# Where the 448-column operands of TensorE lie in SBUF: at multiples of 256 bytes, or 64 bytes behind them

## The chip, the cores and the metric

The kernel runs on one core of one Trainium2 chip. The metric is the device time of one execution, in microseconds. The kernel before took 874.99 us, the median of three runs (873.45 to 876.74).

## The reference

Two layers, each a linear attention block and a dense block, are applied in turn to `x` of 2048 tokens by 448 features; both layers use the same weights. All is float32.

```python
def _A_ref(x, wqkv, wo):                       # 16 heads of 28
    q, k, v = ...                              # x @ wqkv, 448 x 1344
    pq, pk = phi(q), phi(k)                    # where(t > 0, t + 1, exp(t)) + 1e-6
    kv = jnp.einsum("bhsd,bhse->bhde", pk, v)
    z = jnp.einsum("bhsd->bhd", pk)
    num = jnp.einsum("bhqd,bhde->bhqe", pq, kv)
    den = jnp.einsum("bhqd,bhd->bhq", pq, z)[..., None] + 1e-6
    return (num / den) merged @ wo

def _B_ref(x, w1, b1, w2, b2):                 # 448 -> 1792 -> 448
    return gelu(x @ w1 + b1) @ w2 + b2

x = x + _A_ref(_layernorm(x), A_wqkv, A_wo)
x = x + _B_ref(_layernorm(x), B_w1, B_b1, B_w2, B_b2)
# and both once more
```

## The kernel before, in words

**Splitting.** The products are made in the float32r type. Each operand is split into a high part, rounded to that type, and a low part, the rest; a product is then high x high, high x low and low x high. Tiles whose names end in h or hi and l or lo are such pairs (`w1h`/`w1l`, `w2h`/`w2l`, `gh`/`gl`, `kh`/`kl`, `XH`/`XL`, `Mh`/`Ml`).

**Tiling.** The tokens lie in 16 tiles of 128, a tile of `x` being 128 x 448. In the attention block each tile is normalized, transposed by blocks through DRAM (or, for the first tiles, by TensorE) into `XH` and `XL`, and projected to K and Q: 11 matmuls each, with 128 x 128 pieces of XH or XL as the stationary operand and 448 columns of the weights `wk` or `wq` as the moving one (`proj`, L555). The G matmuls (L625) add up the transposed normalized input times phi(K) over all tiles, in four PSUM banks, again with 448 columns of `kh` or `kl` moving. From G, `wv` and `wo` small products give a matrix M (`kv`, `m`), and each output tile is phi(Q) times M: 448 columns of M move (`o`, `oc`; `oc` reads M from the tiles of the used-up `wq`, filled by DMA). In the dense block, blocks of four tiles (512 tokens) are multiplied by `w1`: here 512 columns of XH or XL move, as four runs of 128 (`f_`, L902). Gelu follows on ScalarE, the split on ScalarE and VectorE, and then for each of the 14 pieces of 128 hidden features the product with `w2`: 448 columns of `w2h` or `w2l` move over 128 x 128 pieces of `gh` or `gl` (`y_mm`, L931).

**Order.** The order of the work on all engines is written out by hand: `ORDER` (L15) has for each layer a text of short names with tile numbers, and `run` (L973) issues them one after the other. The prefix `>` marks work of the next layer. Dependencies between engines become semaphore waits by the tiles read and written.

**Buffers.** SBUF tiles come from the pools `consts`, `smalls`, `wts` and `work`, one behind the other. `work` holds rings, one for each tag (`ring`, L167), with as many buffers as `BUFS` (L155) says: H (9 buffers of 448 columns: tiles of x and pieces of wv), S (5 of 1024: staging, spread tiles, the pieces of wo, `Ml`), W0 to W6 and V0 to V6 (pieces of `wk` and `wq`, later phi(Q) and others), E and F (2 each of 512: `kh`, `kl`, `zh`, `zl`, `Mh`, later halves of phi(Q)), A and B (2 each of 512: `gh`, `gl`, `xnh`, `xnl`), e, xn, XH, XL, tail. The pool `wts` holds `w1h`, `w1l`, `w1x`, `w2h`, `w2l`.

**Addresses.** `consts` and `smalls` end at byte 6144 of a partition, which is 24 x 256, and every tile of `wts` and `work` is a multiple of 256 bytes long (448 columns are 7 x 256 bytes, 512 columns 8 x 256). So in the kernel before, every moving and every stationary operand of the matmuls of 448 and of 512 columns starts at a multiple of 256, but for a handful with `ones` or quarters of a tile as the stationary one.

Of the kernel before, what the change touches and what calls it, by code (L numbers as in the profile page):

```python
# [8 lines left out]
F32 = mybir.dt.float32  # L9
F32R = mybir.dt.float32r  # L10
# [111 lines left out]
def linear_attn_mlp_kernel(  # L122
# [15 lines left out]
    S, D = x0.shape  # L138
    F = w1.shape[1]
    H, DH = 16, 28  # L140
    NT = S // 128
    NF = F // 128
    G = 112
# [5 lines left out]
    smalls = ctx.enter_context(tc.tile_pool(name="smalls", bufs=2))  # L149
    wts = ctx.enter_context(tc.tile_pool(name="wts", bufs=1))  # L150
    work = ctx.enter_context(tc.tile_pool(name="work", bufs=2))
    psum = ctx.enter_context(tc.tile_pool(name="psum", bufs=1, space=bass.MemoryType.PSUM))
    ctx.enter_context(tc.manual_schedule())

    BUFS = {"H": 9, "S": 5, "e": 3, "xn": 2, "A": 2, "B": 2, "E": 2, "F": 2, "X": 2, "tail": 2, "small": 2}  # L155
# [5 lines left out]
    def f(ap):  # L161
        return ap.bitcast(F32)
# [2 lines left out]
        return psum.tile([128, 512], F32, name=name, tag=tag, bufs=BANKS[tag])  # L165

    def ring(tag, n, name, dt=F32):  # L167
        return work.tile([128, n], dt, name=name, tag=tag, bufs=BUFS.get(tag, 1))

    def wide(tag):  # L170
        return 512 if tag in ("xn", "W4", "W5") else D
# [32 lines left out]
    w1h = wts.tile([128, 3, F], F32R, name="w1h")  # L204
    w1l = wts.tile([128, 3, F], F32R, name="w1l")
    w1x = wts.tile([128, F], F32R, name="w1x")
    w2h = wts.tile([128, NF, D], F32R, name="w2h")
    w2l = wts.tile([128, NF, D], F32R, name="w2l")

    def rows(t):  # L210
        return slice(t * 128, (t + 1) * 128)
# [1 line left out]
    T = {}  # L213
# [8 lines left out]
    def copy(eng, out, src):  # L222
        if eng is act:
            act.copy(out, src)  # L224
        else:
            eng.tensor_copy(out, src)
# [37 lines left out]
    def load_half(src, h, name):  # L264
        s = ring("S", 1024, name)[:, :2 * D].rearrange("p (c n) -> p c n", c=2)
        if h == 0:
            sp.dma_start(s, src[:256, :].rearrange("(c p) n -> p c n", p=128))
        else:
            sp.dma_start(s[:, 0], src[256:TL, :])
            sp.dma_start(s[:64, 1], src[TL:, :])  # L270
            sp.dma_start(s[64:, 1], src[TL:, :])
        return s

    def wpiece(name, i):
        tag = f"{'W' if name == 'k' else 'V'}{i}"
        return ring(tag, wide(tag), f"w{name}{i}", F32R)[:, :D]

    def wload(name, col):
        def go(l, n, e):
            if l:  # L280
                T[l, "st", name, n] = load_half(wqkv[:, col:col + D], n, "stg")
                return
            if (l, "st", name, n // 2) not in T:
                T[l, "st", name, n // 2] = ring("S", 1024, "stg")[:, :2 * D].rearrange("p (c n) -> p c n", c=2)
            load_piece(wqkv[:, col:col + D], n, T[l, "st", name, n // 2][:, n % 2], ENG[e or "s"])
        return go
# [301 lines left out]

    @op
    def kh(l, t, e):  # L590
        T["kh", l, t] = ring("E", 512, "kh", F32R)[:, :D]
        T["kl", l, t] = ring("F", 512, "kl", F32R)[:, :D]
        act.activation(T["kh", l, t], T["K", l, t], AF.Identity, bias=tiny)

    @op
# [28 lines left out]
    @op  # L624
    def G_(l, t, e):  # L625
        if t == 0:
            T["G", l] = [bank("acc", f"G{c}")[:, :D] for c in range(4)]
        acc = T["G", l]
        h, lo = T["sp", l, t]
        kh, kl = T["kh", l, t], T["kl", l, t]  # L630
        first, last = t == 0, t == NT - 1
        for c in range(4):
            pe.matmul(acc[c], h[:, c * 128:(c + 1) * 128], kh, start=first, stop=False)
        for c in range(4):
            pe.matmul(acc[c], h[:, c * 128:(c + 1) * 128], kl, start=False, stop=last and c == 3)
        for c in range(3):
            pe.matmul(acc[c], lo[:, rows(c)], kh, start=False, stop=last)
# [29 lines left out]

    @op
    def zh(l, n, e):
        T[l, "zh"] = ring("E", 512, "zh", F32R)[:, :D]  # L670
        copy(ENG[e or "a"], T[l, "zh"], T["za", l])

    @op
    def zl(l, n, e):
        T[l, "zl"] = ring("F", 512, "zl", F32R)[:, :D]
        dve.tensor_sub(T[l, "zl"], T["za", l], f(T[l, "zh"]))

    @op
# [56 lines left out]

    @op
    def mh(l, g, e):
        T[l, "Mh", g] = ring("EEFF"[g], 512, "Mh", F32R)[:G, :D]
        copy(ENG[e or "a"], T[l, "Mh", g], T[l, "mp", g])

    @op
# [268 lines left out]
```

## Time and profile before

| | |
|---|---|
| time, median of 3 runs | 874.99 us (873.45 to 876.74) |
| profiled execution, its own time | 874.72 us |
| its span, first to last instruction | 873.0 us |
| TensorE (PE) busy | 99%, 4144 matmuls |
| weight loads (PEld) busy | 88%, 4144 loads |
| VectorE, ScalarE, GpSimd busy | 52%, 41%, 24% |
| granted TensorE clock | 0.999 |

PE rows are matmuls and PEld rows the loads of their stationary operands, which overlap them. Matmuls also overlap one another, and their ends are modelled, so a row's mean length is longer than the distance from one start to the next. In a row that groups instructions, the name after `<-` lists what the instruction reads: first the moving operand, then the stationary one (`y<-w2h,gh` moves w2h over gh, `hp<-XH,w1h` moves XH over w1h). Then come the shape, the count, the busy time of the group, the mean length of one in ns, and the idle time before them with what ended it.

### The profile page before, as it was taken

To read this page: it belongs to the slowest core of one execution; us is meant where nothing else is said; L and a number is where in the kernel's file an instruction comes from. 1 tells how busy PE (TensorE), PEld (TensorE's weight loads), DVE (VectorE), ACT (ScalarE), POOL (GpSimd) and SP (SyncE) were. 2 spreads that over 40 slices of the span, in tenths; PEclk is the share of its full clock that TensorE was granted. 3 is DMA by queue.
4 is the path that set the end of the run, shared out by engine and by line. 5 is a ranking of instruction groups with operands and counts; after the bars stand their busy time and mean duration, and the time that the engine had idled before them with its cause. 6 is when DMAs were issued, how large, how long until landed. Compare 5 with 4: busy or idle time off the path is not lost. (4 is left out here: it accounts for less than half of the span.)

```text
span 873.0 us, 11506 instructions
## 1 busy us (share of the span) xinstructions
PE 865.5 (99%) x4144; PEld 768.3 (88%) x4144; DVE 451.2 (52%) x893; ACT 356.5 (41%) x618; POOL 213.5 (24%) x277
## 2 busy tenths in 40 slices
PE   9999999999999999999999999999999999999998
PEld 7999998898888888888899989879888888888887
DVE  7986786574442442235288757846565414332112
ACT  7667646433223213333355664544142332222222
POOL 4655753434110012000122343232222000310000
PEclk9999999999999999999999999999999999999999
DMA  7685366743242113021154534571612402110101
GB/s 222 208 251 174 117 202 217 219 132 124 75 155 70 40 45 118 1 95 60 48 175 147 195 96 139 163 233 28 207 61 97 133 3 88 60 48 1 43 1 42
DMA packets 66392, 98.93 MB, mean 113 GB/s; under 512 B 9248, under 2 KB 60960, under 8 KB 66336
## 3 DMA queue, kind: packets, MB, share of 16 engines
q1 hardware_dynamic: 64528, 98.20, 35.1%
q8 instruction: 32, 0.52, 0.2%
q10 hardware_dynamic: 1808, 0.01, 0.1%
q14 instruction: 24, 0.20, 0.1%
HBM read 58.27 MB, written 36.70 MB: 109 GB/s over the span
## 5 line engine op out<-in xcount | busy, mean ns | idle before, releaser
L929 DVE TENSOR_TENSOR gl<-g,gh 128x512 fp32r<-128x512 f32 x112 | 77.5, 700 | 260.5 <-ACT gh L224 229.6
L919 ACT ACTIVATE g<-hp,b1s 128x512 f32<-128x512 f32 x112 | 76.6, 688 | 329.9 <-PE hp L914 316.3
L938 PE MATMUL y<-w2h,gh 128*128 128x448 f32 x448 | 163.7, 365 | 0.0
L939 PE MATMUL y<-w2l,gh 128*128 128x448 f32 x448 | 163.6, 365 | 0.0
L909 PE MATMUL hp<-XH,w1h 128*128 128x512 f32 x336 | 131.6, 392 | 1.6 <-ACT g L919 1.6
L910 PE MATMUL hp<-XH,w1l 128*128 128x512 f32 x336 | 131.2, 390 | 0.0
L370 POOL TENSOR_TENSOR brs<-bmv,mhalf 128x1 f32<-128x1 f32 x64 | 36.8, 579 | 330.2 <-DVE bmv L364 325.0
L941 PE MATMUL y<-w2h,gl 128*128 128x448 f32 x448 | 116.8, 365 | 0.0
L913 PE MATMUL hp<-XL,w1h 128*128 128x512 f32 x336 | 94.4, 389 | 0.0
L939 PEld LDWEIGHTS y<-w2l,gh 128*128 128x128 f32 x448 | 84.2, 188 | 8.0
L938 PEld LDWEIGHTS y<-w2h,gh 128*128 128x128 f32 x448 | 84.1, 188 | 8.0
L224 ACT CAST gh<-g 128x512 fp32r<-128x512 f32 x112 | 68.5, 620 | 54.4 <-PE y L939 46.3
L941 PEld LDWEIGHTS y<-w2h,gl 128*128 128x128 f32 x448 | 84.1, 188 | 6.9
L909 PEld LDWEIGHTS hp<-XH,w1h 128*128 128x128 f32 x336 | 63.1, 188 | 14.0 <-ACT g L919 2.0
L913 PEld LDWEIGHTS hp<-XL,w1h 128*128 128x128 f32 x336 | 63.1, 188 | 13.2
L910 PEld LDWEIGHTS hp<-XH,w1l 128*128 128x128 f32 x336 | 63.1, 188 | 11.9
L445 DVE TENSOR_TENSOR XL<-sp,XH 128x512 fp32r<-128x512 f32 x60 | 42.7, 724 | 32.0 <-ACT XH L224 31.7
L773 POOL TENSOR_TENSOR pz<-pq,zb 128x448 f32<-128x448 f32 x32 | 37.8, 1182 | 87.7 <-DMA pq<-pq_d 49.8
L873 POOL TENSOR_TENSOR x<-x,b2b 128x448 f32<-128x448 f32 x32 | 39.6, 1247 | 44.8 <-DVE xm L378 44.8
L552 POOL TENSOR_TENSOR xnl<-x,xnh 128x384 fp32r<-128x384 f32 x32 | 33.0, 1031 | 55.6 <-ACT xnh L224 38.9
L911 PE MATMUL hp<-XH,w1x 128*128 128x512 f32 x112 | 43.6, 389 | 0.0
L914 PE MATMUL hp<-XL,w1x 128*128 128x512 f32 x112 | 43.6, 389 | 0.0
(167 smaller groups left out, 1416.6 us busy)
## 6 DMA issues: line engine op xcount, KB each, us to landing
sq_m<-sq SPq DMA_DIRECT2D x16, 512.0 KB, 2.9
sp<-sq_m SPq DMA_DIRECT2D x64, 128.0 KB, 3.1
x<-in_A_x_dram SPq DMA_DIRECT2D x32, 224.0 KB, 3.3
pq_d<-eq SPq DMA_DIRECT2D x32, 224.0 KB, 3.2
sq_a<-sq SPq DMA_DIRECT2D x14, 512.0 KB, 3.6
sp<-sq_a SPq DMA_DIRECT2D x56, 128.0 KB, 3.1
pq<-pq_d SPq DMA_DIRECT2D x32, 224.0 KB, 3.1
x<-x_d SPq DMA_DIRECT2D x32, 224.0 KB, 3.0
```

What stands on the lines that cost most here:

```text
L224: act.copy(out, src)
L445: dve.tensor_sub(squares(lo), spread_tile(kind, l, t), f(squares(hi)))
L909: pe.matmul(o, w1h[:, c, s], x.moving(x.hi, c), start=(c == 0), stop=False)
L910: pe.matmul(o, w1l[:, c, s], x.moving(x.hi, c), start=False, stop=False)
L911: pe.matmul(o, w1x[:, s], x.moving(x.hi, 3), start=False, stop=False)
L913: pe.matmul(o, w1h[:, c, s], x.moving(x.lo, c), start=False, stop=False)
L914: pe.matmul(o, w1x[:, s], x.moving(x.lo, 3), start=False, stop=True)
L919: act.activation(T[l, "g", n], T[l, "hp", n], AF.Gelu_apprx_tanh, bias=b1s[:, n % NF:n % NF + 1])
L929: dve.tensor_sub(lo, T[l, "g", n], f(hi))
L938: pe.matmul(o, gh[:, r], w2h[:, i], start=first, stop=False)
L939: pe.matmul(o, gh[:, r], w2l[:, i], start=False, stop=False)
L941: pe.matmul(o, gl[:, r], w2h[:, i], start=False, stop=last)
```

## The change

A new pool `mov` stands behind `work`. The rings with tags that begin with H, S, V or W move into it, and so do `w2h` and `w2l`, which leave `wts`. The first tile of `mov` is a gap of 16 columns of float32 (64 bytes), and everything behind it is a multiple of 256 bytes long; so all tiles of `mov` start 64 bytes behind a multiple of 256. The tiles `kh`, `kl`, `zh`, `zl` and `Mh`, in the rings E and F (still in `work`), use the columns 16 to 463 of their 512 instead of 0 to 447, which puts them 64 bytes behind, too. `qh` and `ql` in E and F are stationary and stay at column 0. XH, XL, `gh`, `gl`, `xnh`, `xnl`, `w1h`, `w1l` and `w1x` stay at multiples of 256.

A few operands are carried along with their rings: the tiles of x and of phi(Q) that TensorE transposes, and the pieces of `wv`, are stationary and now lie 64 bytes further on; the staging tiles in H, S and W, which DMAs fill, do as well. The instructions, their order, the tags and the number of buffers of each are the same as before.

```diff
@@ -149,6 +149,7 @@
     work = ctx.enter_context(tc.tile_pool(name="work", bufs=2))
+    mov = ctx.enter_context(tc.tile_pool(name="mov", bufs=1))
@@ -165,7 +166,8 @@
     def ring(tag, n, name, dt=F32):
-        return work.tile([128, n], dt, name=name, tag=tag, bufs=BUFS.get(tag, 1))
+        home = mov if tag[0] in "HSVW" else work
+        return home.tile([128, n], dt, name=name, tag=tag, bufs=BUFS.get(tag, 1))
@@ -204,8 +206,9 @@
-    w2h = wts.tile([128, NF, D], F32R, name="w2h")
-    w2l = wts.tile([128, NF, D], F32R, name="w2l")
+    mov.tile([128, 16], F32, name="gap", tag="gap", bufs=1)
+    w2h = mov.tile([128, NF, D], F32R, name="w2h", tag="w2h", bufs=1)
+    w2l = mov.tile([128, NF, D], F32R, name="w2l", tag="w2l", bufs=1)
@@ -588,8 +591,8 @@
-        T["kh", l, t] = ring("E", 512, "kh", F32R)[:, :D]
-        T["kl", l, t] = ring("F", 512, "kl", F32R)[:, :D]
+        T["kh", l, t] = ring("E", 512, "kh", F32R)[:, 16:16 + D]
+        T["kl", l, t] = ring("F", 512, "kl", F32R)[:, 16:16 + D]
@@ -667,12 +670,12 @@
-        T[l, "zh"] = ring("E", 512, "zh", F32R)[:, :D]
+        T[l, "zh"] = ring("E", 512, "zh", F32R)[:, 16:16 + D]
...
-        T[l, "zl"] = ring("F", 512, "zl", F32R)[:, :D]
+        T[l, "zl"] = ring("F", 512, "zl", F32R)[:, 16:16 + D]
@@ -735,7 +738,7 @@
-        T[l, "Mh", g] = ring("EEFF"[g], 512, "Mh", F32R)[:G, :D]
+        T[l, "Mh", g] = ring("EEFF"[g], 512, "Mh", F32R)[:G, 16:16 + D]
```

## The prediction

> **What bounds the kernel now.** I read the page's engine shares first, then the waits of PE, then PE's instructions grouped by form, and last the timeline of single matmuls.
>
> ```profile
> span 873.0 us, 11506 instructions
> PE 865.5 (99%) x4144; PEld 768.3 (88%) x4144; DVE 451.2 (52%) x893; ACT 356.5 (41%) x618; POOL 213.5 (24%) x277
> PEclk9999999999999999999999999999999999999999
> ```
> ```profile
> PE hp L909 <- ACT g L919: 1.6, 1, 1.6
> PE hot L241 <- POOL ones L180: 1.1, 1, 1.1
> PE psk L560 <- DVE kl L597: 0.4, 1, 0.4
> ...
> PE psQ L504 <- ACT wq L224: 0.2, 1, 0.2
> ```
>
> TensorE is busy for 865.5 of 873.0 us, at the full clock, and its listed waits come to about 4 us. So the span is the number of matmuls times the spacing of their starts, and only a change of that spacing can move it. How many of each kind there are:
>
> ```profile
> L938 PE MATMUL y<-w2h,gh 128*128 128x448 f32 x448 | 163.7, 365 | 0.0
> L939 PE MATMUL y<-w2l,gh 128*128 128x448 f32 x448 | 163.6, 365 | 0.0
> L909 PE MATMUL hp<-XH,w1h 128*128 128x512 f32 x336 | 131.6, 392 | 1.6 <-ACT g L919 1.6
> L910 PE MATMUL hp<-XH,w1l 128*128 128x512 f32 x336 | 131.2, 390 | 0.0
> L941 PE MATMUL y<-w2h,gl 128*128 128x448 f32 x448 | 116.8, 365 | 0.0
> L913 PE MATMUL hp<-XL,w1h 128*128 128x512 f32 x336 | 94.4, 389 | 0.0
> L911 PE MATMUL hp<-XH,w1x 128*128 128x512 f32 x112 | 43.6, 389 | 0.0
> L914 PE MATMUL hp<-XL,w1x 128*128 128x512 f32 x112 | 43.6, 389 | 0.0
> L560 PE MATMUL psq<-wq,XH 128*128 128x448 f32 x180 | 41.6, 367 | 0.0
> L560 PE MATMUL psk<-wk,XH 128*128 128x448 f32 x180 | 41.6, 366 | 0.4 <-DVE kl L597 0.4
> L844 PE MATMUL op<-wq,qh 128*128 128x448 f32 x144 | 33.1, 365 | 0.0
> L633 PE MATMUL G<-kh,xnh 128*128 128x448 f32 x128 | 31.7, 368 | 0.1
> L635 PE MATMUL G<-kl,xnh 128*128 128x448 f32 x128 | 31.4, 367 | 0.0
> ...
> L706 PE MATMUL kvp<-gt,wvt 128*112 128x112 f32 x64 | 6.7, 263 | 0.3 <-ACT gt L224 0.3
> L241 PE MATMUL hot<-ones 128*128 128x512 f32 x12 | 4.9, 581 | 1.1 <-POOL ones L180 1.1
> L798 PE MATMUL tq<-ident,pq 128*112 128x128 f32 x32 | 4.8, 272 | 0.0
> ```
>
> The matmuls of 512 columns are 3 x 336 + 2 x 112 = 1232 (and 12 warm-up ones). From 4144 I take these, 64 of `kvp`, 32 of `tq` and the 16 transposes of the first four tiles (4 halves of 2, 2 tiles of 4, in the order list): **2788 matmuls have 448 columns**, and these are the ones whose moving operand is shifted.
>
> A record is longer than the spacing, since matmuls overlap. The timeline gives the spacing (start, length, line, count in a run):
>
> ```profile
> 701.24 0.84 PE L913 MATMUL hp<-XL,w1h 128*128 128x512 f32 x3
> 701.92 0.39 PE L914 MATMUL hp<-XL,w1x 128*128 128x512 f32 x1
> 702.15 0.36 PE L938 MATMUL y<-w2h,gh 128*128 128x448 f32 x1
> 702.35 0.37 PE L939 MATMUL y<-w2l,gh 128*128 128x448 f32 x1
> 702.56 0.36 PE L938 MATMUL y<-w2h,gh 128*128 128x448 f32 x1
> ...
> 703.77 0.97 PE L941 MATMUL y<-w2h,gl 128*128 128x448 f32 x4
> 704.58 0.39 PE L909 MATMUL hp<-XH,w1h 128*128 128x512 f32 x1
> ```
>
> From 701.24 to 702.15 there are four matmuls of 512 columns: 227 ns each, and the record of one is 389, so a record is about 162 ns longer than the spacing. From 702.15 to 704.58 there are twelve of 448 columns (eight alternating on L938 and L939, four on L941): 202.5 ns each, record 365, again 162 more. The 448s are not even: the first starts 0.20 us before the second, the second 0.21 before the third. So some take 0.20 and others 0.21, on the same line and tiles, while the 512s repeat their 227. Nothing waits there; the beat comes from within PE or its reads.
>
> The beat is also not the only pace. Here are the same forms in two stretches of the attention part, 66 to 98 us first (its window row, then two forms), 440 to 505 us second:
>
> ```profile
> 66.00:98.00 32.00, 32.00 (x156) 29.08 (x155) 19.22 (x32) 24.33 (x47) 21.29 (x24) 1.00 0.53 158
> L560 PE MATMUL psk<-wk,XH 128*128 128x448 f32 x38 | 9.0, 368 | 0.0
> L633 PE MATMUL G<-kh,xnh 128*128 128x448 f32 x32 | 7.9, 368 | 0.0
> ```
> ```profile
> L560 PE MATMUL psk<-wk,XH 128*128 128x448 f32 x66 | 15.2, 365 | 0.0
> L633 PE MATMUL G<-kh,xnh 128*128 128x448 f32 x38 | 9.3, 365 | 0.0
> ```
>
> In the first stretch every form is at 368, in the second at 365: identical instructions, PE without a gap, full clock. So the spacing depends on something beside the column count, a phase between two streams that can lock in a slower position. That is what makes an effect of the address credible here; it doesn't say in which direction 64 bytes push it.
>
> **The change part by part.** It issues no new instruction, moves none, changes no order and no number of buffers, so no wait is added and no queue is passed. What differs is addresses. *Tiles of H, S, V, W now in their own pool, with E and F used from column 16:* the moving operands go from 0 to 64 bytes past a multiple of 256; this is the whole effect and is costed below. *Other engines' accesses to those tiles:* at the same count I cost them at nothing. They lie beside PE: in the stretch where they are fullest DVE is busy 122.7 of 170 us, which leaves 47 us of cover.
>
> ```profile
> 30.00:200.00 170.00, 170.00 (x843) 153.47 (x842) 122.67 (x247) 98.83 (x178) 86.66 (x102) 1.00 0.61 192
> x<-x_d SPq DMA_DIRECT2D x32, 224.0 KB, 3.0
> ```
>
> Even a tenth more on DVE would be 12 us there, still hidden. *DMAs into H, S and W:* a load lands after 3.0 us and PE's list of waits names no DMA; a seventh more (one more 256-byte piece on the seven of a row) would be 0.4 us on a load that nobody waits for. *Stationary operands that move too* (`pq` under `tq`, `wvt` under `kvp`, the first tiles): 112 matmuls; even at 4 ns each 0.4 us, taken as zero.
>
> Now the 2788. The trace of before has no 448 at 64 bytes, so I bound its spacing by rows. *From below:* by columns alone a 448 would take 227 x 448/512 = 198.6 ns, against 202.5 now: 4 ns less, or 11 us over all. *From above:* the locked stretch, 368 instead of 365: 3 ns more, 8 us; the longest of the beat, 0.37 instead of 0.365, says at most 5 ns, 14 us. Between these I take **200 ns, the 0.20 us that the beat's shortest member reaches already** (702.15 to 702.35): if the shift takes away what makes the beat, each matmul keeps that pace. That is 2.7 ns below the beat's mean of about 202.7 (365 less 162.3): 2788 x 2.7 = 7.5 us. The locked stretches gain 3 ns more: 156 matmuls in the one shown, 0.5 us. Where 448s give way to 512s, L909 and L910 run at 392 and 390 instead of 389 (336 x 3 + 336 x 1 = 1.3 us); I count none of it and keep it as a bound. Against this, a PE that is 1% faster meets some waits earlier; of the 4 us of waits I add 0.5 us. The sum is 7.5 + 0.5 - 0.5 = 7.5 us.
>
> The profiled execution took 874.72 us, a span of 873.0 and 1.7 around it; the median of the three runs, 874.99, lies 0.3 above. **874.7 - 7.5 = 867.2 us.**
>
> The Trainium skill, "TensorE: Matmul & The Clock Gate" (Part 1), puts a column at 1/2.4 ns, so 213.3 ns for 512 and 186.7 for 448; the trace then has 13.7 ns of fixed cost on a 512 and 15.8 on a 448, and with the 512's cost a 448 would take 200.4, an estimate that gives 868. By that it agrees with the pace chosen.
>
> **The rivals.** *No change* (874.7): the moving read doesn't care about 64 bytes and the beat is one of PE's own clocking. For it: the beat runs on unchanged over tiles that lie at different places (w2h and w2l on neighbouring lines, wk and kh in the stretch at 365). Against it: the same instructions run at 365 and at 368. The Trainium skill's "SBUF — State Buffer" (section "Who interferes with whom") speaks for it: PE has two read ports of its own and waits on nobody, so a shift between the moving and the stationary read could not matter; the two paces of this trace are not explained by it.
>
> *Slower, the shift locks the slow pace* (about 885): the phase that 66 to 98 us shows becomes the usual one, since the moving read now always starts one 64-byte step out of line with the stationary read. Place: every 448-column matmul. Price: 368.5 less 365 (0.37 us records in the timeline of the beat, 368 in the locked stretch), 3.5 x 2788 = 9.8 us, 884.5. It decides as soon as more than about half of the matmuls sit at 368, since the other half's gain of 2.7 no longer pays. Worse is possible if each operand now touches eight 256-byte pieces instead of seven and pays for the eighth as for 64 columns, 389 - 365 = 24 ns or 67 us; against that, a partial piece would have to cost a full one.
>
> *Much faster, the fixed part goes* (about 835): the beat is only the visible rest of a collision between the moving read and the load of the next weights, and the shift ends it. The nearest row for a floor is the load itself:
>
> ```profile
> L938 PEld LDWEIGHTS y<-w2h,gh 128*128 128x128 f32 x448 | 84.1, 188 | 8.0
> ```
>
> At 188 ns per matmul the gain is 14.5 x 2788 = 40 us. Against it: the 512s, at multiples of 256 throughout, hold 227 without a beat, so an even pace needn't mean a smaller fixed part. The Trainium skill's "TensorE: Matmul & The Clock Gate" (Part 1) gives 448/2.4 + 2.5 = 189.2 ns for matmuls back to back, an estimate of 837; no row here shows such a spacing.
>
> **How the numbers follow.** Even pace at about 200 ns: 0.52, its own range 863 to 871. No change: 0.24. Locked slow or a further piece paid: 0.14. Fixed part partly or wholly gone (835 to 860): 0.10. The range 857 to 886 takes in the bounds of 11 us down and 10 us up with some room for waits, and leaves out most of the last case and the costly half of the third, near 0.16. About 0.5% (870.6 to 879.4 around the median) is what a measurement of this kernel tells from no change. Faster: nearly all of 0.52 and the 0.10, so 0.60; within: 0.24 and a little, 0.26; slower: 0.14.
>
> **What would show it.** The beat: records of L938, L939 and L941 all at 362 or so instead of 365, with starts 0.20 us apart; the attention stretch at 66 to 98 us no longer at 368. No change: 365 and the mix of 0.20 and 0.21 stay. Slow lock: 368 or more on all 448 forms. Fixed part gone: 355 or less. L913 and the other 512s should stay at 389. Wrong in its whole manner would be a time that moves while these lengths don't: then new waits of PE, on DVE or on a DMA, would have to stand in its list.

## The result and the profile after

The changed kernel takes 869.95 us (median of six executions, 868.45 to 871.31), the kernel before beside it 875.56 us: a ratio of 0.9939, with a 95% interval of 0.9922 to 0.9955. So it is faster by 0.6%: 5.3 us by the ratio, 5.6 by the two medians. The forecast of 867.2 lies 2.75 us below the measured time. The profiled execution took 869.59 us.

The page and the groups of PE by form, of the changed kernel (line, what is written and read, shape, count, busy time, mean ns of one, idle time before; L941, L942 and L944 are the lines 938, 939 and 941 of before):

```profile
span 867.8 us, 11506 instructions
PE 860.4 (99%) x4144; PEld 767.7 (88%) x4144; DVE 452.7 (52%) x893; ACT 356.5 (41%) x618; POOL 214.4 (25%) x277
...
L941 PE MATMUL y<-w2h,gh 128*128 128x448 f32 x448 | 162.4, 362 | 0.0
L942 PE MATMUL y<-w2l,gh 128*128 128x448 f32 x448 | 162.1, 362 | 0.0
...
L916 PE MATMUL hp<-XL,w1h 128*128 128x512 f32 x336 | 94.4, 389 | 0.0
...
L563 PE MATMUL psk<-wk,XH 128*128 128x448 f32 x180 | 41.1, 363 | 0.4 <-DVE kl L600 0.4
```

The 448s went from 365 to 362 ns, and the 512s of L916 (L913 before) stayed at 389. The attention stretch that ran at 368 before is at 362 now (groups from 66 to 98 us, changed kernel):

```profile
L563 PE MATMUL psk<-wk,XH 128*128 128x448 f32 x41 | 9.3, 362 | 0.0
L638 PE MATMUL G<-kl,xnh 128*128 128x448 f32 x32 | 7.7, 362 | 0.0
L636 PE MATMUL G<-kh,xnh 128*128 128x448 f32 x32 | 7.7, 362 | 0.0
```

The timeline has a run of 512s, twelve 448s, and the next 512 (start in us, length in us, line, count):

```profile
696.88 0.84 PE L916 MATMUL hp<-XL,w1h 128*128 128x512 f32 x3
697.56 0.39 PE L917 MATMUL hp<-XL,w1x 128*128 128x512 f32 x1
697.78 0.37 PE L941 MATMUL y<-w2h,gh 128*128 128x448 f32 x1
697.99 0.36 PE L942 MATMUL y<-w2l,gh 128*128 128x448 f32 x1
698.19 0.36 PE L941 MATMUL y<-w2h,gh 128*128 128x448 f32 x1
...
699.39 0.96 PE L944 MATMUL y<-w2h,gl 128*128 128x448 f32 x4
700.19 0.39 PE L912 MATMUL hp<-XH,w1h 128*128 128x512 f32 x1
```

The first 448 after a 512 takes 0.21 us; from 697.99 to 700.19 come eleven more, 200.0 ns each. In the starts, the beat of before, five matmuls long (199 and 207 ns, then three of 202 or 203, mean 202.7), has become one of three (201, 202, 197, mean 200.0).

Where the 5.2 us between the spans (873.0 and 867.8) come from, counted by the distances of neighbouring starts: the 448s that follow one another without a wait (gaps under 215 ns, some 2670 of them) have a mean distance of 203.0 ns before and 200.3 after, 2670 x 2.74 = 7.3 us; the same on the 67 or so steps from a 448 to a 512 gives 0.2. So 2.3 us were lost elsewhere: 0.2 to the 512s, and nearly all the rest to waits and the start. The list of PE's waits in the changed kernel (total us, times, longest):

```profile
PE hot L244 <- POOL ones L182: 1.1, 1, 1.1
PE hp L912 <- ACT XH L227: 0.7, 2, 0.4
PE kvp L709 <- DMA wvt<-in_A_wqkv_dram: 0.5, 1, 0.5
PE psk L563 <- DVE kl L600: 0.4, 1, 0.4
PE psq L563 <- DVE eq L578: 0.4, 1, 0.4
PE hp L912 <- ACT g L922: 0.4, 1, 0.4
PE psQ L507 <- ACT wq L227: 0.2, 1, 0.2
```

Of these, the two on the copy XH, the one on a piece of `wv` and the one of the Q projection on VectorE's `eq` do not stand in the list of before. In total the list has 3.7 us here and 3.9 before, since the one wait of 1.6 us on `g` has shrunk to 0.4. So the list does not show the loss: it counts only the time in which no matmul has an open record, and a record runs some 160 ns past the next start. The wait on `eq` is 0.37 us in the list and 0.53 between the starts. The distances of the starts show the loss.

### The profile page after: what moved, and what is told of

Read it like the earlier page. It is cut to its first block, busy times and chain, and to the rows that moved or that the text cites. A ratio compares the mean times of both kernels' runs of the same rounds, so it can differ in the third digit from the quotient of the medians.

```text
span 867.8 us, 11506 instructions
## 1 busy us (share of the span) xinstructions
PE 860.4 (99%) x4144; PEld 767.7 (88%) x4144; DVE 452.7 (52%) x893; ACT 356.5 (41%) x618; POOL 214.4 (25%) x277
## 4 chain that ended last, share of the span: by engine, by line
PE 75%; DMA 3%; DVE 3%; POOL 1%; issue 1%; ACT 1%; SPq 1%; POOLq 0%; ACTq 0%; DVEq 0%
PE y L944 10%; PE y L941 10%; PE y L942 10%; PE hp L912 8%; PE hp L913 8%; PE hp L916 8%; PE op L847 3%; PE hp L914 3%; PE hp L917 3%; PE op L850 2%; PE psk L563 1%; PE psq L563 1%; DMA sp<-sq_m 1%; PE G L636 1%; PE G L638 1%
## 5 line engine op out<-in xcount | busy, mean ns | idle before, releaser
L932 DVE TENSOR_TENSOR gl<-g,gh 128x512 fp32r<-128x512 f32 x112 | 78.0, 704 | 257.6 <-ACT gh L227 229.4
L941 PE MATMUL y<-w2h,gh 128*128 128x448 f32 x448 | 162.4, 362 | 0.0
L942 PE MATMUL y<-w2l,gh 128*128 128x448 f32 x448 | 162.1, 362 | 0.0
L913 PE MATMUL hp<-XH,w1l 128*128 128x512 f32 x336 | 131.5, 391 | 0.0
L944 PE MATMUL y<-w2h,gl 128*128 128x448 f32 x448 | 115.7, 362 | 0.0
L916 PE MATMUL hp<-XL,w1h 128*128 128x512 f32 x336 | 94.4, 389 | 0.0
L941 PEld LDWEIGHTS y<-w2h,gh 128*128 128x128 f32 x448 | 84.0, 187 | 7.5
L942 PEld LDWEIGHTS y<-w2l,gh 128*128 128x128 f32 x448 | 84.0, 188 | 7.3
L944 PEld LDWEIGHTS y<-w2h,gl 128*128 128x128 f32 x448 | 83.9, 188 | 5.5
L916 PEld LDWEIGHTS hp<-XL,w1h 128*128 128x128 f32 x336 | 63.1, 188 | 13.2
L913 PEld LDWEIGHTS hp<-XH,w1l 128*128 128x128 f32 x336 | 63.1, 188 | 12.1
```

What stands on the lines that cost most here:

```text
L913: pe.matmul(o, w1l[:, c, s], x.moving(x.hi, c), start=False, stop=False)
L916: pe.matmul(o, w1h[:, c, s], x.moving(x.lo, c), start=False, stop=False)
L932: dve.tensor_sub(lo, T[l, "g", n], f(hi))
L941: pe.matmul(o, gh[:, r], w2h[:, i], start=first, stop=False)
L942: pe.matmul(o, gh[:, r], w2l[:, i], start=False, stop=False)
L944: pe.matmul(o, gl[:, r], w2h[:, i], start=False, stop=last)
```

## The experiments

Theory at the outset: the **distance** of the moving operand from the stationary one, modulo 256 bytes, sets the spacing. Rivals: the new **place** of the tiles does it, or the moving operand's own **address**. In each run the mean distance of neighbouring starts of 448s without a wait is given as its spacing.

### The new layout without the 64 bytes

```diff
-    mov.tile([128, 16], F32, name="gap", tag="gap", bufs=1)
-        T["kh", l, t] = ring("E", 512, "kh", F32R)[:, 16:16 + D]
+        T["kh", l, t] = ring("E", 512, "kh", F32R)[:, :D]
...
```

> The new order of the buffers stays, the 64 bytes go: no gap tile, and kh, kl, zh, zl, Mh start at column 0. Distance theory (the distance of the moving operand from the stationary one modulo 256 bytes sets the pace): records of the 448-column matmuls back at 365 to 368 ns, about 875 us. Rival, place theory (it is the new place of w2 and of the rings that helps): 362 ns as in the changed kernel, about 870 us.

874.72 us, a ratio of 1.0007 (0.9993 to 1.0022) to the kernel before; spacing 203.0 ns. From the groups of this run:

```profile
L940 PE MATMUL y<-w2h,gh 128*128 128x448 f32 x448 | 163.6, 365 | 0.0
L562 PE MATMUL psk<-wk,XH 128*128 128x448 f32 x180 | 41.6, 367 | 0.4 <-DVE kl L599 0.4
```

All is as before the change. The place theory falls.

### Everything shifted by 64 bytes

```diff
+    wts.tile([128, 16], F32, name="gap")
     w1h = wts.tile([128, 3, F], F32R, name="w1h")
```

(in the kernel before)

> The kernel before with one gap of 64 bytes ahead of the weights: moving and stationary operands, those of 512 columns too, all lie 64 bytes behind a multiple of 256; their distance is 0 as before. Distance theory: nothing changes, 365 ns for 448 columns, 389 for 512, about 875 us. Rival, address theory (the moving operand's own address modulo 256 counts, whatever the stationary one's is): 362 ns for 448 columns and about 870 us, or another time if the 512s change too.

875.99 us, a ratio of 1.0019 (1.0008 to 1.0031):

```profile
L939 PE MATMUL y<-w2h,gh 128*128 128x448 f32 x448 | 163.7, 365 | 0.0
L910 PE MATMUL hp<-XH,w1h 128*128 128x512 f32 x336 | 131.8, 392 | 1.2 <-ACT g L920 0.8 <-ACT XH L225 0.4
```

The moving operands lie 64 bytes behind a multiple of 256, as in the changed kernel, and nothing is gained. The own address alone isn't it. The time is even 0.2% longer, some 1.7 us, and the interval leaves out 1. In the trace more matmuls are in stretches at the slow pace (at least six gaps in a row of 206 or 207 ns): 510 here, 227 before, which raises the mean spacing to 203.4; 283 x 4 ns is 1.1 us. One trace of each does not tell whether that belongs to the kernel or to the execution.

### Distance 64 from the other side

```diff
-    mhalf = consts.tile([128, 1], F32, name="mhalf")
+    cst = consts.tile([128, 3], F32, name="cst")
+    mhalf, tiny, zc = cst[:, 0:1], cst[:, 1:2], cst[:, 2:3]
```

(in the changed kernel, `tiny` and `zc` as tiles of their own go; all behind them starts 64 bytes earlier)

> Distance 64 made from the other side: the moving operands of 448 columns lie at multiples of 256 again, and everything stationary lies 192 bytes behind one (three one-column constants share a tile, so that the weights and rings start 64 bytes earlier; the gap ahead of w2 and the moving rings then brings these back to a multiple of 256). XH and XL move at 192 over w1 at 192, distance 0 as before. Distance theory: 362 ns for 448 columns, 389 for 512, about 870 us. Rival, address theory (the moving operand's own address counts): 365 ns and about 875 us, since the moving operands lie as in the kernel before.

869.75 us, a ratio of 0.9943 (0.9927 to 0.9959); spacing 200.3 ns:

```profile
L940 PE MATMUL y<-w2h,gh 128*128 128x448 f32 x448 | 162.4, 362 | 0.0
L915 PE MATMUL hp<-XL,w1h 128*128 128x512 f32 x336 | 94.5, 389 | 0.0
```
```profile
PE psq L562 <- DVE eq L577: 0.4, 1, 0.4
```

The moving operands of 448 columns are back at multiples of 256, the stationary ones at 192, and the gain is the whole one. With the two runs above, the distance is shown to decide the spacing of the 448s, not the place of the tiles nor the moving operand's own address. The wait on VectorE's `eq` is there again.

### The other distances

The gap and the columns of E and F were changed together, for 128 bytes:

```diff
-    mov.tile([128, 16], F32, name="gap", tag="gap", bufs=1)
+    mov.tile([128, 32], F32, name="gap", tag="gap", bufs=1)
-        T["kh", l, t] = ring("E", 512, "kh", F32R)[:, 16:16 + D]
+        T["kh", l, t] = ring("E", 512, "kh", F32R)[:, 32:32 + D]
...
```

and in the same way 48 columns for 192 bytes, 8 for 32, 24 for 96, 40 for 160 and 56 for 224.

> The moving operands of 448 columns lie 128 bytes behind a multiple of 256 instead of 64 (gap of 32 columns, E and F used from column 32). If only lying in line with the stationary operand is bad, records at 362 ns and about 870 us, as with 64. If each 64-byte step has its own phase, another length, between 355 and 369 ns, and a time between 850 and 886 us.

> The same with 192 bytes (gap of 48 columns, E and F from column 48). If only lying in line is bad, 362 ns and about 870 us; if each step has its own phase, another length than at 64 or 128, between 355 and 369 ns.

> The moving operands of 448 columns lie 32 bytes behind a multiple of 256 (gap of 8 columns, E and F from column 8). If the reads go by pieces of 64 bytes, the phase is that of distance 0 with a split first piece: 365 ns or more and 875 us or more. If only the distance in time counts, a value between those of 0 and 64: 362 to 366 ns, 870 to 875 us.

> Moving operands of 448 columns 96 bytes behind a multiple of 256 (gap of 24 columns, E and F from column 24). Half-step theory (a start in the middle of a 64-byte piece locks every matmul at the slow pace, as 32 did): 369 ns, 882 to 886 us. Rival, a smooth course over the distance: between the lengths at 64 and 128, 362 to 366 ns, 870 to 877 us.

> The same at 160 bytes (gap of 40 columns, E and F from column 40). Half-step theory: 369 ns, 882 to 886 us. Smooth course: between the lengths at 128 and 192, 364 to 366 ns, 874 to 877 us.

> The same at 224 bytes (gap of 56 columns, E and F from column 56). Half-step theory: 369 ns, 882 to 886 us. Smooth course: between the lengths at 192 and at 0, 364 to 366 ns, 873 to 876 us.

Each ratio is to the kernel before run beside it, whose medians were 874.6 to 875.6 us.

| distance, bytes | spacing of 448s, ns | spacing of 512s, ns | median, us | ratio to before (95%) |
|---|---|---|---|---|
| 0 (before) | 203.0 | 227.9 | 875.56 | 1 |
| 32 | 206.4 | 228.2 | 883.60 | 1.0105 (1.0084 to 1.0126) |
| 64 (the change) | 200.3 | 228.0 | 869.95 | 0.9939 (0.9922 to 0.9955) |
| 96 | 205.4 | 227.9 | 882.09 | 1.0078 (1.0063 to 1.0093) |
| 128 | 203.9 | 227.9 | 877.56 | 1.0032 (1.0020 to 1.0045) |
| 160 | 202.7 | 228.4 | 875.21 | 0.9997 (0.9985 to 1.0009) |
| 192 | 202.2 | 229.2 | 874.12 | 0.9996 (0.9985 to 1.0007) |
| 224 | 204.4 | 229.2 | 880.25 | 1.0065 (1.0045 to 1.0085) |

The same form in the runs at 32, 96, 128, 192 and 224 bytes, one fence each:

```profile
L941 PE MATMUL y<-w2h,gh 128*128 128x448 f32 x448 | 165.3, 369 | 0.0
```
```profile
L941 PE MATMUL y<-w2h,gh 128*128 128x448 f32 x448 | 164.7, 368 | 0.0
```
```profile
L941 PE MATMUL y<-w2h,gh 128*128 128x448 f32 x448 | 164.1, 366 | 0.0
```
```profile
L941 PE MATMUL y<-w2h,gh 128*128 128x448 f32 x448 | 163.3, 364 | 0.0
```
```profile
L941 PE MATMUL y<-w2h,gh 128*128 128x448 f32 x448 | 164.0, 366 | 0.0
```

The time follows the spacing: at 32 bytes 2788 x 3.4 = 9.5 us are due, and the ratio of 1.0105 is 9.2. With the 512s counted too (2788 times the change of the one spacing plus 1232 times that of the other), the sum agrees with the measured ratio to within 0.7 us at all distances but 64, where the gain falls 2.1 us behind it.

Lying out of line is no gain in itself; 64 is the only distance of the eight that is clearly faster. At 32 bytes the first expectation held (365 ns or more) and the value between those of 0 and 64 failed. The half-step theory nearly held at 96 (882.09 us, but 368 ns) and failed at 160 and 224. The smooth course failed at 96, held at 160, and at 224 held in the length and failed in the time. Neither rule stands, and the course over the distance is left as a table. In the run at 160 both paces occur with one and the same layout and the same instructions, 122 to 130 us first, 480 to 492 us second:

```profile
L563 PE MATMUL psq<-wq,XH 128*128 128x448 f32 x22 | 5.1, 363 | 0.0
L564 PE MATMUL psq<-wq,XH 128*128 128x448 f32 x4 | 1.4, 362 | 0.0
```
```profile
L563 PE MATMUL psq<-wq,XH 128*128 128x448 f32 x6 | 1.4, 368 | 0.0
L564 PE MATMUL psq<-wq,XH 128*128 128x448 f32 x2 | 0.7, 368 | 0.0
```

The starts of this run show how it changes over. From 429 to 455 us the 448s stand 200.0 ns apart. Then PE waits half a microsecond for `eq`, and behind that wait they stand 206.7 apart, up to the next wait at 515 us. So the distance sets which paces are possible, and where several are, a stretch mostly stays at one until a wait or another kind of matmul breaks it. There are exceptions: in the kernel before, a slow stretch begins near 643 us without a wait.

### The 512s at a distance

```diff
-    w1h = wts.tile([128, 3, F], F32R, name="w1h")
+    still.tile([128, 32], F32, name="gap2")
+    w1h = still.tile([128, 3, F], F32R, name="w1h")
...
```

(`w1l` and `w1x` alike; `still` is a new last pool. With 16 columns of gap instead of 32 the distance is 128.)

> The changed kernel, and w1 moves behind all else to 192 bytes past a multiple of 256, so that XH and XL (at 0) move at a distance of 64 from it. If 64 is a better distance for any matmul, the 512-column forms fall below 389 ns; if 0 is right for 512 columns, they rise to between 390 and 396 ns, 1232 x 1 to 7 ns, and the time to between 871 and 879 us. The 448s stay at 362.

> The changed kernel with w1 behind all else at 128 bytes past a multiple of 256, so that XH and XL move at a distance of 128 from it. Distance theory with 0 the best for 512 columns: their spacing is longer than the 228 ns of the changed kernel by 1 to 7 ns, 871 to 879 us. If 128 suits them, below 228 ns and below 869 us. The 448s stay at 362.

Neighbouring 512s start 228.0 ns apart in the changed kernel, 229.4 at 64 and 232.5 at 128. The times are 870.83 us (0.9951, 0.9938 to 0.9965), just below the expected 871, and 875.59 us (1.0003, 0.9990 to 1.0017). One form in the run at 64, then at 128, 389 in the changed kernel:

```profile
L918 PE MATMUL hp<-XL,w1h 128*128 128x512 f32 x336 | 95.1, 391 | 0.0
```
```profile
L918 PE MATMUL hp<-XL,w1h 128*128 128x512 f32 x336 | 96.2, 394 | 0.0
```

By the spacing 0 is the best of the three: 1232 x 4.5 ns = 5.5 us at 128 undo the whole change. The time at 64 alone can't be told from that of the changed kernel. That `w1` lies elsewhere was not tried without the shift.

The 512s also account for the time at 192 bytes. In that run they stood 229.2 apart instead of 227.9, though their own operands lie as before, and 1232 x 1.3 = 1.6 us of the 2.2 that the 448s gained were lost there. The loss lies in the first ten of each run of 512s, behind the 448s: 230.9 ns there against 228.6 before, and from the eleventh on 226.8 against 226.7. In the two kernels with w1 elsewhere the later ones are longer, too, 229.0 and 232.7. That at 192 bytes they start in another phase after the 448s would fit; no run tried it.

### Half of the change

```diff
-        home = mov if tag[0] in "HSVW" else work
-        return home.tile([128, n], dt, name=name, tag=tag, bufs=BUFS.get(tag, 1))
+        return work.tile([128, n], dt, name=name, tag=tag, bufs=BUFS.get(tag, 1))
...
```

(E and F from column 0 again; only `w2h` and `w2l` stay in `mov`)

> Only w2h and w2l lie 64 bytes behind; all rings, E and F are as before. The three w2 forms at 362 ns, the attention forms at 365 to 368. Theory (each matmul gains by its own pair of operands, and the attention part's gain is partly given back to waits on ScalarE and VectorE): 1344 x 2.7 = 3.6 us gained and no new wait, about 871 us, at most 2 us behind the whole change. Rival (nothing is given back, the gain goes by count): 1344 of 2788, half of the change's gain, about 872.5 us, and the other half with the attention part.

873.47 us, a ratio of 0.9975 (0.9963 to 0.9988). Both expectations missed, the rival by 1 us, mine by 2.5. The dense part did what was expected, the attention part did not stay as it was. The first row is the dense form, then two attention forms from 66 to 98 us:

```profile
L940 PE MATMUL y<-w2h,gh 128*128 128x448 f32 x448 | 162.4, 362 | 0.0
```
```profile
L562 PE MATMUL psk<-wk,XH 128*128 128x448 f32 x41 | 9.6, 368 | 0.0
L635 PE MATMUL G<-kh,xnh 128*128 128x448 f32 x32 | 7.9, 368 | 0.0
```

The dense 448s have a spacing of 200.4 instead of 202.7, so each matmul goes by its own pair of operands. The attention ones rose from 203.3 to 204.0, as 463 gaps lie in slow stretches instead of 227. By the spacing the dense part gains 1344 x 2.3 = 3.1 us and the attention part loses 1444 x 0.75 = 1.1 us, which leaves 2.0, close to the 2.2 of the ratio. But that does not explain the median: the traced execution took 875.44 us, the longest of the ten that the median is of, and its span is 0.7 us longer than that of before. New waits stand in it, on `xnh`, on `x` and on a piece of `wv`, 0.6 to 0.9 us each, against the expectation of none. Whether the slow stretches and these waits belong to this kernel or to that execution stays open, and so does how the gain of the whole change divides between the two parts.

## Why the prediction was right, and where not

**The bound.** Right: TensorE's spacing times the number of matmuls moved the time, and the times of the six further distances follow it, to within 0.7 us with the 512s counted.

**The pace of 200 ns.** Right in the number, 200.0 in undisturbed stretches. The reason given for it, that the beat goes and each matmul keeps the pace of its fastest member, was wrong: a beat remains, from 197 to 202 ns, only its mean is lower, and the record of 362 that was to be shown by every matmul is again a mean. The fastest member of before stood at 199, so that the new mean came out at the 0.20 read off it is luck. With the first 448 after each 512 at 206 or 207, the mean spacing is 200.3, so that 7.3 us came of the forecast 7.5 + 0.5 for beat and slow stretches. The slow stretch did vanish, and with it its share. The estimate with the 512's fixed cost, 200.4 by the column time of the Trainium skill's "TensorE: Matmul & The Clock Gate" (Part 1), agrees with the measured 200.3; that the 448s at other distances take 202.2 to 206.4 shows that this cost is not fixed.

**The 512s.** The prediction took them to hold 227 ns without a beat, and used that against the much faster case. The trace of before shows it only from the eleventh of a run on, 226.7 on the mean; the first ten take 228.6, as its own rows at 392 and 390 say.

**The waits.** This is the term that was mis-sized: 0.5 us were set against an earlier PE, and 2.3 us were lost in the profiled execution, 2.1 of them at waits and the start. That the loss goes with the pace is seen in the other kernels: in the three others with the 448s at 200.3 the measured gain falls 1.4 to 2.5 us behind the sum of the two spacings, and in all the rest the time stays within 0.7 us of it. The step that failed is thus to size the term by the 4 us of waits in the list of before: a PE that comes earlier meets waits that this list doesn't have. One piece of it is settled: the gap before the Q projections at 453 us, 0.53 us and 0.11 at the next matmul, stands in all four kernels with the 448s at 200.3 (the change, distance 64 from the other side, and both with w1 elsewhere) and in the one at 160 bytes, whose dense part runs at 201.4; it stands in none of the other nine, the kernel before among them. The waits at the start, near 134 and 562 us on XH, and on a piece of `wv` come and go between kernels of one pace, so which of them make up the rest stays open.

**Accesses of the other engines, DMAs, stationary operands moved along.** Costed at nothing, and rightly as far as it shows: VectorE is busy for 452.7 us against 451.2. With all shifted by 64 bytes, the DMA tiles among it, the ratio was 1.0019, some 1.7 us, of which slow stretches make up 1.1. The list of waits names a DMA now, against the claim that nobody waits for a load; the kernel with the new layout and no shift has the same wait of 0.5 us, so it does not need the 64 bytes.

**The rivals.** No change would have needed a spacing that doesn't care about the distance. The Trainium skill's "SBUF — State Buffer" (section "Who interferes with whom") speaks for it with two read ports of PE, independent of each other, and a PE that waits on nobody. The prediction drew from this that the shift could not matter; the table above, from 200.3 to 206.4 ns, disagrees, and the measurement decides. The slow lock was a real case with the wrong distance: at 32 bytes nearly every matmul sits at 369 ns, and the 884.5 us worked out for it compares with 883.60. Its dearer case, 24 ns for an eighth piece of 256 bytes, was seen at no distance: the most is 3.4 ns. That a start out of line with the stationary operand would bring it at 64 was not so. The much faster case was seen at no distance that was tried: no mean spacing fell below 200.3 ns.

**Open.** Shown is that the distance sets the spacing; why it does is not. That two reads of SBUF meet is an inference from the distance; no row of the profile shows a read being held up. Finer steps than 32 bytes were not tried.

## What to carry to other kernels

When PE is busy throughout and one kind of matmul repeats, compare its record lengths between stretches: identical instructions at 365 and at 368 ns are a sign that the spacing has several possible paces. Then the distance of moving and stationary operand is a knob worth a row of trials in steps of 32 bytes, separately for each column count: here a wrong step cost more than the right one brought (9 us at 32 bytes against 5 at 64). A gain on the busiest engine is to be discounted by the waits that it will meet earlier; the profile's list of its waits doesn't show them beforehand. Here some 2 us of 7.5 were lost so.

## What the runs showed of the hardware

Matmuls of 448 float32r columns over 128 x 128 stationary pieces, each with its own weight load, started 200.3, 202.2, 202.7, 203.0, 203.9, 204.4, 205.4 or 206.4 ns apart on the mean, as the moving operand's start address lay 64, 192, 160, 0, 128, 224, 96 or 32 bytes behind the stationary one's, modulo 256. Shifting both together by 64 left them at 203.4, with more matmuls at the slow pace. Those of 512 columns, read as four runs of 128, took 228.0, 229.4 and 232.5 ns at distances of 0, 64 and 128, and 229.2 at distance 0 where the 448s ahead of them were at 192 or 224. At distances 0 and 160 the same instructions hold either of two paces, 202.7 or 206.7 and 200.0 or 206.7 ns, for tens of microseconds.
